# Placing score tiles by the matmuls of their own row half

## The chip, the cores and the metric

The kernel runs on one core of a Trainium2 chip. The metric is the device time of one execution in microseconds; the time before is the median of three runs.

## The reference

The input `x` has 2048 tokens of width 512. It is normalised per token (no scale, no shift), and two branches work on the result:

```python
xn = layernorm(x)
qkv = xn @ wqkv                        # 32 heads of width 16
s = softmax(q @ k.T / 4) @ v @ wo      # attention, then projection
g = silu(gelu(xn @ w1 + b1) @ w2 + b2) # 1376 hidden columns
out = x + s * g
```

All inputs are float32. The projections and both layers of the gated branch are made of three matmuls for each product: high times high, high times low, and low times high part of the operands.

## The kernel before, in words

The work runs in three parts, one after the other on TensorE.

The **first part** normalises `x`, transposes it, and makes some of the value and query/key tiles with 128-row matmuls.

The **middle part**, called the 64-row part here, makes the rest of the values, queries and keys and the whole gated branch. Its contractions are cut into halves of 64 rows: half 0 of the array (rows 0 to 63) and half 1 (rows 64 to 127) each take their own stream of matmuls, and both accumulate into the same PSUM tiles in turn. `run` issues these products in steps: in each step it raises `prog["n"]`, and for each half `a` it first calls `fill(a)` and then `mm(a, ...)`. There are 1488 steps, so each half gets 1488 product matmuls. A list `plan`, made ahead, orders the pieces: `quad` (values), `half` (first layer, queries and keys) and `down` (second layer).

`fill(a)` places the **score tiles**. Before the softmax can be taken, the row maxima of all scores are needed, and the kernel computes them in a pass of its own: `s_one(a)` takes the next tile for half `a`, `s_mm` makes 128 x 512 scores with one matmul of 48 rows in that half, and `s_max` reduces them on VectorE to two maxima per row. Such a tile takes one of two PSUM buffers (`ps_a`, `ps_b`) from the ring `s_ring`, in turn; a tile can be started when the reduction of the tile two before it has released the buffer. `4 * LEAD` = 576 score tiles are placed in the 64-row part, 288 on each half, half 0 and half 1 in turn (that is what `made[0] <= made[1]` decides). The remaining 1472 are made in the last part.

When 64 tiles of a unit (four heads, 512 queries) are done, `s_end0` reduces the maxima once more on VectorE, and some tiles later the place of one score tile is taken by `s_end1` and `s_end2`: a small transpose with all 128 rows in a buffer of the same ring (L252), a copy on ScalarE (L258), and a DMA on SP. This happens eight times in the 64-row part. `s_end0` also asks for the loads of queries two units ahead.

When a product accumulates into a PSUM tile that the other half wrote last, `mm` needs a proof that this write is over. `prog["seen"]` holds how far that is known: `taken()` raises it with each score tile (the third one back must be over), and where this is not enough, `mark()` puts a one-element instruction on ScalarE (L569) for which the matmul then waits. `SLOTS` = 1470 is the step at which the last score tile is to be placed, `FILL0` = 84 the step before which none is.

The **last part** runs the attention: transposed scores, exponentials on ScalarE, products with the values, the rest of the score tiles, and the output projection.

Of the kernel before, what the change touches and what calls it, by code (L numbers as in the profile page):

```python
# [32 lines left out]
LEAD = 144  # L33
# [3 lines left out]
FILL0 = 84  # L37
# [10 lines left out]
def fused(ctx: ExitStack, tc: tile.TileContext, x, wqk, wv, wo, w1, b1, w2, b2, out):  # L48
# [105 lines left out]
    made = [0, 0]  # L154
# [3 lines left out]
    def tick():  # L158
        for e in later:
            e[0] -= 1  # L160
# [31 lines left out]
    def s_whole(job, a):  # L192
        ps = s_tile()[0]
        s_mm(ps, job, a, 0, 0, CH)
        s_max(ps, job, a, slice(0, 2))

    def s_one(a):
        made[a] += 1
        s_whole(heads[made[a] - 1], a)
# [48 lines left out]
    prog = {}  # L248

    def s_end1(u):  # L250
        pm = s_tile()[0] if "seen" in prog else t_tile()
        nc.tensor.matmul(pm[:2 * GH * NCH, :P], NM.pop(u).rearrange("p i a -> p (i a)"), ident_r, start=True, stop=True)  # L252
        MH[u] = pm

    def s_end2(u):
        mh = qring.tile([2 * GH * NCH, P], F32, name="mh", bufs=1)
        if "seen" in prog:
            nc.scalar.activation(mh, MH.pop(u)[:2 * GH * NCH, :P], AF.Copy)  # L258
        else:
            nc.vector.tensor_copy(mh, MH.pop(u)[:2 * GH * NCH, :P])  # L260
        nc.sync.dma_start(mh_d[u].rearrange("i j (q s) -> (i j q) s", s=P), mh)
        sent.add(u)
# [33 lines left out]
    for j in range(len(pairs)):  # L296
        for h in range(2):
# [4 lines left out]
            due = next((i for i in range(j, len(pairs)) if is_m[i]), len(pairs))  # L302
# [4 lines left out]
            n = 2 if nd < len(parts) and parts[nd][2] and ready - nd > room else 1  # L307
            n = max(n, need - 2 * (left - 1))
# [215 lines left out]

    prog.update(n=0, pe=0, seen=0)
    writer = {}
    s_when = []
    ndown = sum(1 for e in plan if e[0] == "down")
    SLOTS = 12 * (4 * VQ + 2 * len(pairs)) + 6 * ndown - 18

    def fill(a):
        due = 4 * LEAD * (prog["n"] - FILL0) // (SLOTS - FILL0)
        if sum(made) < min(due, 4 * LEAD) and (made[0] <= made[1]) == (a == 0):
            taken()
            if later and later[0][0] <= 0:
                u = later.pop(0)[1]
                s_end1(u)
                s_end2(u)
                return
            s_one(a)  # L540
            tick()

    def taken():
        prog["pe"] += 1
        s_when.append(prog["pe"])
        if len(s_when) > 2:
            prog["seen"] = max(prog["seen"], s_when[-3])

    def mm(a, key, ps, lhs, rhs, first, last):
        r = slice(64 * a, 64 * a + 64)  # L550
        token = None
        if not first and writer[key][0] != a and writer[key][1] > prog["seen"]:
            if not tokens or tokens[-1][0] < writer[key][1]:
                mark()
            prog["seen"], token = next(x for x in tokens if x[0] >= writer[key][1])
        i = nc.tensor.matmul(ps, lhs[r], rhs[r], start=first, stop=last).ins  # L556
        if token is not None:
            tc.add_manual_dep(i, token, SYNC, reason="other row tile")
        prog["pe"] += 1
        latest[0] = (prog["pe"], i.name)  # L560
        writer[key] = (a, prog["pe"])

# [2 lines left out]
    def mark(dve=False):  # L565
        if dve:
            i = nc.vector.tensor_copy(junk[:, 1:], ident_r[:1, :1].bitcast(F32)).ins
        else:
            i = nc.scalar.activation(junk[:, :1], ident_r[:1, :1].bitcast(F32), AF.Copy).ins  # L569
        tc.add_manual_dep(i, latest[0][1], SYNC, reason="row tile done")  # L570
        tokens.append((latest[0][0], i.name))
# [7 lines left out]
    def run(ops, hooks={}):  # L579
        for n, two in enumerate(zip(*ops)):  # L580
            prog["n"] += 1
            for a in range(2):
                fill(a)
                mm(a, *two[a])
            for h in hooks.get(n, []):
                h()
# [321 lines left out]
    for t in range(NW):  # L908
        n = DONE + 2 * t
# [6 lines left out]
    for i, t in enumerate(late):  # L916
        n = L - 2 * len(late) - 1 + 2 * i
# [86 lines left out]
```

## Time and profile before

| | |
|---|---|
| median of 3 runs (lowest, highest) | 1636.11 us (1634.83, 1637.08) |
| the profiled execution: its time / its span | 1635.62 us / 1633.7 us |
| busy share of the span: TensorE, VectorE, ScalarE, GpSimd | 98%, 86%, 77%, 23% |
| granted TensorE clock | 0.998 |
| 64-row part: first and last product matmul | 52.9 us, 491.5 us |
| score tiles in it: number, first and last | 576, 72.7 us, 486.6 us |
| products of the 64-row part: mean record of a matmul | 0.39 us |

The record of a matmul lasts from its start to its modelled end; matmuls overlap, so the distance between starts, and not the record, tells the rate. L180 is the matmul of a score tile, L186 its reduction, L556 the products of the 64-row part, L252 the transpose of `s_end1`. PEld rows are weight loads; each matmul has its own.

### The profile page before, as it was taken

How to read it: one execution, taken by the hardware profiler on the slowest of the kernel's cores; microseconds unless marked ns; L12 is line 12 of the kernel's file. 1: busy time of each engine (PE TensorE's matmuls, PEld its weight loads, DVE VectorE, ACT ScalarE, POOL GpSimd, SP SyncE). 2: the span in 40 equal slices, each digit the busy share in tenths (PEclk: the TensorE clock that was granted, in tenths of full speed). 3: DMA queues.
4: the chain of work that ended last, by engine and by line, in shares of the span. 5: the costliest groups of instructions: out<-in, count | busy, mean ns of one | idle time of the engine just before them, and what ended most of it. 6: DMA issues, size and time to landing. Idle time of an engine off the chain costs nothing.

```text
span 1633.7 us, 32521 instructions
## 1 busy us (share of the span) xinstructions
PE 1605.2 (98%) x12146; PEld 928.8 (57%) x12146; DVE 1406.8 (86%) x2330; ACT 1255.7 (77%) x2522; POOL 371.8 (23%) x366
## 2 busy tenths in 40 slices
PE   9999999999999999999999999999999999999998
PEld 7899998999994444444444444444444444444445
DVE  7299999999988999999999999999999999999733
ACT  4333333434339999999999999999999999999884
POOL 4235565755640001001100200100010000000144
PEclk9999999999999999999999999999999999999999
DMA  6625333454322113111411411321131111110152
GB/s 200 148 65 156 103 127 97 146 143 123 110 82 72 41 28 70 29 35 40 78 32 26 67 41 28 59 39 29 34 69 27 28 29 41 29 32 18 57 191 94
DMA packets 76222, 116.93 MB, mean 72 GB/s; under 512 B 24964, under 2 KB 26244, under 8 KB 74696
## 3 DMA queue, kind: packets, MB, share of 16 engines
q1 hardware_dynamic: 72604, 102.42, 22.9%
q0 software_dynamic: 3264, 12.35, 3.9%
q8 instruction: 96, 1.57, 0.4%
q14 instruction: 62, 0.51, 0.1%
q10 hardware_dynamic: 196, 0.07, 0.0%
HBM read 84.35 MB, written 25.97 MB: 68 GB/s over the span
## 4 chain that ended last, share of the span: by engine, by line
PE 92%; ACT 4%; DVE 2%; issue 1%; DMA 0%; ACTq 0%; POOL 0%; SPq 0%; DVEq 0%; POOLq 0%
PE ps L773 21%; PE ps L180 14%; PE pst L704 14%; PE ps L556 12%; PE pv L773 8%; PE pst L556 7%; PE ps L704 5%; PE ps L79 3%; PE pv L180 3%; ACT slot L706 3%; PE pv L556 2%; PE pst L79 1%; DVE os L780 1%; ACT os L779 1%; DVE slot L74 0%
## 5 line engine op out<-in xcount | busy, mean ns | idle before, releaser
L186 DVE TENSOR_REDUCE mx<-ps 128x2 f32<-128x512 f32 x1685 | 1096.9, 685 | 121.7 <-PE ps L180 80.3
L706 ACT ACTIVATE slot<-pst 128x512 f32<-128x512 f32 x1533 | 833.7, 606 | 29.4 <-PE pst L704 18.2
L773 PE MATMUL ps<-slot,vsb 128*32 128x512 f32 x2944 | 392.1, 605 | 0.0
L704 PE MATMUL pst<-qt,kt 50*128 50x512 f32 x1149 | 378.2, 429 | 0.4 <-DVE gt L637 0.3
L180 PE MATMUL ps<-kt,slot 48*128 48x256 f32 (+1 forms) x1036 | 325.2, 374 | 8.2 <-DVE os L780 8.2
L706 ACT ACTIVATE slot<-ps 128x512 f32<-128x512 f32 x515 | 311.5, 606 | 21.0 <-PE pst L704 13.7
L704 PEld LDWEIGHTS pst<-qt,kt 50*128 50x128 f32 x1149 | 182.9, 184 | 243.2 <-ACT slot L706 239.1
L186 DVE TENSOR_REDUCE mx<-pv 128x2 f32<-128x512 f32 x363 | 248.1, 684 | 18.5 <-PE pv L180 14.0
L556 PE MATMUL ps<-slot,w1h 64*128 64x512 f32 x1088 | 234.2, 394 | 0.4 <-ACT junk L569 0.4
L180 PE MATMUL ps<-kt,qz 48*128 48x512 f32 x512 | 218.9, 429 | 0.3 <-ACT mh L258 0.3
L180 PEld LDWEIGHTS ps<-kt,slot 48*128 48x128 f32 x1036 | 170.3, 184 | 38.1 <-DVE os L780 15.2
L556 PEld LDWEIGHTS ps<-slot,w1h 64*128 64x128 f32 x1088 | 159.9, 185 | 9.1 <-ACT junk L569 1.9
L704 PE MATMUL ps<-qt,kt 50*128 50x512 f32 x387 | 162.7, 422 | 0.0
L556 PE MATMUL ps<-slot,w1l 64*128 64x512 f32 x544 | 159.7, 393 | 0.0
L773 PE MATMUL pv<-slot,vsb 128*32 128x512 f32 x1152 | 153.2, 604 | 0.8 <-DVE gx L866 0.8
L180 PE MATMUL ps<-slot,slot 48*128 48x256 f32 (+1 forms) x442 | 140.4, 375 | 3.7 <-DVE os L780 3.1
L360 POOL TENSOR_TENSOR hl<-hg,hh 128x512 fp32r<-128x512 f32 x76 | 96.8, 1295 | 135.7 <-ACT hh L359 79.9
L180 PE MATMUL pv<-kt,slot 48*128 48x512 f32 (+1 forms) x328 | 123.1, 375 | 3.1 <-DVE os L780 3.0
L569 ACT ACTIVATE junk<-ident_r 1x1 f32<-1x1 f32 x90 | 17.7, 196 | 134.1 <-PE pst L556 128.4
L704 PE MATMUL pst<-qt,slot 50*128 50x512 f32 x384 | 119.1, 423 | 0.0
L704 PEld LDWEIGHTS ps<-qt,kt 50*128 50x128 f32 x387 | 71.2, 184 | 67.5 <-ACT slot L706 52.8
L773 PEld LDWEIGHTS ps<-slot,vsb 128*32 128x32 f32 x2944 | 57.9, 108 | 84.0 <-issue 83.7
(165 smaller groups left out, 2085.5 us busy)
## 6 DMA issues: line engine op xcount, KB each, us to landing
raw<-in_w SPq DMA_DIRECT2D x88, 256.0 KB
qk_h<-hh SPq DMA_DIRECT2D x32, 256.0 KB
qk_l<-hl SPq DMA_DIRECT2D x32, 256.0 KB
qt<-qk_h SPq DMA_DIRECT2D x128, 64.0 KB
slot<-qk_h SPq DMA_DIRECT2D x92, 64.0 KB
xt<-in_x SPq DMA_DIRECT2D x16, 256.0 KB
g_d<-gt POOLq DMA_DIRECT2D x16, 256.0 KB, 3.7
qt<-qk_l SPq DMA_DIRECT2D x64, 64.0 KB
```

The costliest lines, as they stand in the source:

```text
L79: nc.tensor.matmul(ps, lhs[a], rhs[b], start=first and n == 0, stop=last and n == 2)
L180: return nc.tensor.matmul(ps[:, c0:c0 + w], QS[u][r, p, qi * P:(qi + 1) * P], kts[u // NCH % KB][p][r, k0:k0 + w], start=True, stop=True).ins
L186: nc.vector.tensor_reduce(MX[u][:, 2 * p:2 * p + 2, qi, ki][:, heads, parts], ps.rearrange("p (n c) -> p n c", c=HC), axis=AX.X, op=OP.max)
L360: nc.gpsimd.tensor_sub(hl, raw, hh.bitcast(F32))
L556: i = nc.tensor.matmul(ps, lhs[r], rhs[r], start=first, stop=last).ins
L569: i = nc.scalar.activation(junk[:, :1], ident_r[:1, :1].bitcast(F32), AF.Copy).ins
L704: nc.tensor.matmul(ps, kts[g % KB][p][r, k * P:(k + 1) * P], QT[u][r, p, :], start=True, stop=True)
L706: nc.scalar.activation(PT[u, k][:, 2 * p + a, :], ps, AF.Exp, scale=SCALE)
L773: nc.tensor.matmul(PV[u][32 * j:32 * j + 32, :], vsb[:, k, h:h + 32], PT[u, k][:, j, :], start=(k == 0), stop=(k == NT - 1))
L779: nc.scalar.activation(OS[u][:, :HC], pv[:, :HC], AF.Copy)
L780: nc.vector.tensor_copy(OS[u][:, HC:], pv[:, HC:])
```

## The change

`fill(a)` decides in a different unit when the next tile is due. Before, the number of tiles that should have been placed is worked out from the step: 576 spread evenly over the steps from 84 to 1470. After, `row[a]` counts every matmul given to half `a`, products and score tiles alike, and `put` counts the places taken (score tiles and the transposes of `s_end1`). A tile may be placed on half `a` when `row[a]` has reached a due count that starts at 84 and rises by (1470 + 288 - 84) / (576 + 9) = 2.86 with each place taken. The order of the halves, the number of tiles and their work stay as they are.

```diff
-    s_when = []
+    s_when, put, row = [], [0], [0, 0]
     ndown = sum(1 for e in plan if e[0] == "down")
     SLOTS = 12 * (4 * VQ + 2 * len(pairs)) + 6 * ndown - 18
 
     def fill(a):
-        due = 4 * LEAD * (prog["n"] - FILL0) // (SLOTS - FILL0)
-        if sum(made) < min(due, 4 * LEAD) and (made[0] <= made[1]) == (a == 0):
+        due = FILL0 + put[0] * (SLOTS + 2 * LEAD - FILL0) // (4 * LEAD + LEAD // 16)
+        if sum(made) < 4 * LEAD and row[a] >= due and (made[0] <= made[1]) == (a == 0):
             taken()
+            put[0] += 1
             if later and later[0][0] <= 0:
                 u = later.pop(0)[1]
                 s_end1(u)
                 s_end2(u)
                 return
             s_one(a)
+            row[a] += 1
             tick()
...
         prog["pe"] += 1
+        row[a] += 1
         latest[0] = (prog["pe"], i.name)
         writer[key] = (a, prog["pe"])
```

## The prediction

> **What bounds the kernel now.** I read the page first, for what is busy; then busy time by stretch and the chain, for the 64-row part; then the groups and waits of that part; then the timeline, one score tile at a time.
>
> ```profile
> PE 1605.2 (98%) x12146; PEld 928.8 (57%) x12146; DVE 1406.8 (86%) x2330; ACT 1255.7 (77%) x2522; POOL 371.8 (23%) x366
> ```
>
> ```profile
> 52.80:491.60 438.80, 438.17 (x3565) 397.19 (x3564) 383.34 (x597) 160.21 (x363) 237.55 (x203) 1.00 0.41 116
> ```
>
> ```profile
> 206.33 0.70 PE ps L556 x6
> ```
>
> TensorE never rests, and in the stretch of the 64-row part (second fence: PE, PEld, DVE, ACT, POOL) it is busy 438.17 of 438.80 us. That hides a loss. The two row halves run side by side: in the chain six products take 0.70 us, three for each half, so a matmul occupies its half for one slot of 0.233 us. Each half has 1488 products, 288 score tiles and 8 transposes of `s_end1`: 1784 slots, 416.3 us. The stretch is 438.8 us long. Each half loses 22.5 us in gaps that the other half covers, so no view of idle time shows them. The attention part follows in order on the same engine; a microsecond lost by both halves here moves the end by one.
>
> Where is it lost? The groups of the stretch in which score tiles are made, and the waits:
>
> ```profile
> L186 DVE TENSOR_REDUCE mx<-ps 128x2 f32<-128x512 f32 x576 | 378.9, 689 | 60.5 <-PE ps L180 35.8 <-PE ps L556 7.3 <-PE pst L556 4.9
> ...
> L180 PE MATMUL ps<-kt,qz 48*128 48x512 f32 x512 | 218.9, 429 | 0.3 <-ACT mh L258 0.3
> ```
>
> ```profile
> PEld ps L180 <- DVE mx L186: 4.2, 15, 0.3
> PEld ps L556 <- ACT junk L569: 1.9, 5, 0.8
> ```
>
> VectorE needs 378.9 us for its 576 reductions in 415 us: not the bound. But a score tile's record is 429 ns on average, where a product's is 390: some start before their weights are in. The timeline has the reason:
>
> ```profile
> 73.11 0.69 DVE L186 TENSOR_REDUCE mx<-ps 128x2 f32<-128x512 f32 x1 [28.61 <-PE ps L180]
> ...
> 75.92 1.43 DVE L186 TENSOR_REDUCE mx<-ps 128x2 f32<-128x512 f32 x2
> ...
> 200.23 1.29 DVE L186 TENSOR_REDUCE mx<-ps 128x2 f32<-128x512 f32 x2 [0.27 <-PE ps L556]
> ```
>
> ```profile
> 76.66 0.18 PEld L180 LDWEIGHTS ps<-kt,qz 48*128 48x128 f32 x1
> ```
>
> ```profile
> 72.69 0.39 PE L180 MATMUL ps<-kt,qz 48*128 48x512 f32 x1
> ...
> 73.15 0.39 PE L180 MATMUL ps<-kt,qz 48*128 48x512 f32 x1
> ...
> 74.09 0.39 PE L180 MATMUL ps<-kt,qz 48*128 48x512 f32 x1
> ...
> 74.60 0.50 PE L180 MATMUL ps<-kt,qz 48*128 48x512 f32 x1
> ...
> 75.49 0.39 PE L180 MATMUL ps<-kt,qz 48*128 48x512 f32 x1
> ...
> 76.11 0.39 PE L180 MATMUL ps<-kt,qz 48*128 48x512 f32 x1
> ...
> 76.66 0.50 PE L180 MATMUL ps<-kt,qz 48*128 48x512 f32 x1
> ...
> 77.50 0.40 PE L180 MATMUL ps<-kt,qz 48*128 48x512 f32 x1
> ...
> 79.64 0.49 PE L180 MATMUL ps<-kt,qz 48*128 48x512 f32 x1
> ...
> 80.94 0.49 PE L180 MATMUL ps<-kt,qz 48*128 48x512 f32 x1
> ```
>
> ```profile
> 480.23 0.41 PE L180 MATMUL ps<-slot,qz 48*128 48x512 f32 x1
> ...
> 481.06 0.39 PE L180 MATMUL ps<-slot,qz 48*128 48x512 f32 x1
> ...
> 481.66 0.41 PE L180 MATMUL ps<-slot,qz 48*128 48x512 f32 x1
> ...
> 482.47 0.39 PE L180 MATMUL ps<-slot,qz 48*128 48x512 f32 x1
> ...
> 482.98 0.49 PE L180 MATMUL ps<-slot,qz 48*128 48x512 f32 x1
> ...
> 484.48 0.40 PE L180 MATMUL ps<-slot,qz 48*128 48x512 f32 x1
> ...
> 485.27 0.44 PE L180 MATMUL ps<-slot,qz 48*128 48x512 f32 x1
> ...
> 485.88 0.43 PE L180 MATMUL ps<-slot,qz 48*128 48x512 f32 x1
> ...
> 486.62 0.49 PE L180 MATMUL ps<-slot,qz 48*128 48x512 f32 x1
> ```
>
> The tile at 75.49 is reduced from 75.92 for 0.69 us, to 76.61. The tile two later, at 76.66, takes the same buffer; its weight load starts at 76.66, 0.05 after the reduction, and the matmul with it. Its record is 0.50 instead of 0.39: the weights are 0.11 us late, and its half loses that. So a buffer is free 0.43 + 0.69 + 0.05 = 1.17 us after its tile's start at best, and the next user wants it 0.11 before its own slot, at 1.28. Two tiles that share a buffer sit on the same half. What matters is the number of own-half slots between them: 6 slots are 1.40 us, enough; 5 slots are 1.17 us, at least 0.11 short.
>
> **The change in counts.** Before, tiles are 1386/576 = 2.41 steps apart, so 2 or 3. In own-half slots that is 2 or 3 from a tile of half 0 to one of half 1, and one more (3 or 4) on the way back, because the tile of half 0 counts itself. After, each place is 2.86 slots after the last one, both ways: mostly 3, sometimes 2, never 4. Stepping both rules through the plan gives, for each tile, the last two distances:
>
> - 3 and 3: 216 before, 397 after
> - 2 then 4, 4 then 2: 117 and 117 before, none after
> - 2 then 3: 54 before, 81 after; 3 then 2: 54 before, 80 after
> - at a transpose of `s_end1`: 24 before (distances 3, 4, 0, 3) and 24 after (3, 5, 2, 3)
>
> The old rule looks rougher, but a 2 is mostly followed by a 4: again 6 slots, the half's reuse distance is kept. Only 108 tiles have 5. The new rule is more even, yet 161 tiles have 5. The reason is in the mean: 2.86 against 2.91, since the transposes now get full distances of their own and the tiles between them move together.
>
> **The prices.** For every score tile of the trace I take the time from the matmul before it on its half to the one after it, less two slots. The quoted rows are the first and the last of each group (two before, one after: 72.69 to 74.09, 480.23 to 481.66 for 2 then 4; 73.15 to 74.60, 481.06 to 482.47 for 4 then 2; 75.49 to 76.66, 481.66 to 482.98 for 2 then 3; 76.11 to 77.50, 484.48 to 485.88 for 3 and 3; 79.64 to 80.94, 485.27 to 486.62 for 3 then 2). The means: 3 and 3, 0.035 us (216 tiles); 2 then 4, 0.020 (101) and 4 then 2, 0.007 (101); 2 then 3, 0.205 (54); 3 then 2, 0.202 (54). Apart stand the 32 tiles just behind a unit's end, 4.4 us in all:
>
> ```profile
> 118.83 0.29 DVE L238 TENSOR_REDUCE nmh<-mx 128x16 fp32r<-128x128 f32 x1
> 119.03 0.28 DVE L238 TENSOR_REDUCE nm<-mx 128x16 f32<-128x128 f32 x1
> ```
>
> These two reductions push back the ones behind them, eight times, under either rule: 4.4 us stay. The 24 places around the transposes cost 2.1 us:
>
> ```profile
> 126.58 0.25 PE L252 MATMUL ps<-ident_r,nmh 128*32 128x128 f32 x1
> ```
>
> ```profile
> 126.87 0.27 ACT L258 ACTIVATE mh<-ps 32x128 f32<-32x128 f32 x1 [1.52 <-PE ps L252]
> ```
>
> The transpose's buffer is free 0.56 us after its start (127.14). Before, the next user comes 3 slots (0.70) later, after it 5 slots (1.17); the other two reuse distances become 8 and 7. So these 2.1 us go, if ScalarE answers as here; if not, up to 2.1 come back.
>
> Before, both halves together: 216 x 0.035 + 101 x 0.020 + 101 x 0.007 + 54 x 0.205 + 54 x 0.202 + 4.4 + 2.1 = 38.6 us, of the 45 lost. After: 365 x 0.035 (32 of the 397 stand for the tiles behind unit ends) + 81 x 0.205 + 80 x 0.202 + 4.4 = 49.8 us.
>
> Waits for the other half's writes rise from 12 to 15 (ScalarE marks from 90 to 93, hidden: ScalarE is busy 160 of 439 us). By the waits view four of them took 1.9 - 0.8 = 1.1 us, 0.28 each; three more cost 0 to 0.8 us, I take 0.4. `s_end1` and `s_end2` come five steps earlier, with their DMA and the query loads that `s_end0` asks for on SP, which are used two units (about 308 steps) later: nothing. The first tile comes two steps earlier, 0.47 us at most if its operands have just landed; the last four earlier, and nobody waits for its buffer before step 1482: nothing. The clock stays at 1.00.
>
> Sum: 49.8 + 0.4 - 38.6 = 11.6 us over both halves, and as neither half can run away from the other, 5.8 us for each. The profiled execution took 1635.6 us (span 1633.7), so 1641.4 by its own time; the median of the runs shown is 1636.1, 0.5 higher: **1641.9 us**.
>
> Bounds: a tile with 5 slots costs at least 0.11 (worked out above) and at most about 0.25 (79.64 to 80.94 is 1.30, 0.14 past 5 slots, and 0.11 for the weights); one with 6 slots costs between 0 and, in the mean, 0.035.
>
> **Rivals.** *Even arrivals are what VectorE needs (faster).* Reductions of 0.64 us each (two in 1.29) fit into even distances of 0.70, the queue on VectorE is gone, every release comes at 1.17: 5 slots cost 0.11, 6 nothing. Then 161 x 0.11 + 4.4 = 22.1 against 38.6, 8.2 us less for each half: 1627.9. It decides if releases come by 1.17. Against it: 3 and 3 occurs 216 times now, and costs 0.035 there.
>
> *Runs of threes become cheap (no difference).* A 2 now makes both halves late in turn, and the threes behind it start with slack, like the 2 and 4 pairs now (mean 0.0135). Then 365 x 0.0135 + 32.8 + 4.4 + 0.4 = 42.5, 2.0 us per half: 1638.1.
>
> *Place in the stream decides (slower yet).* If the halves did not run ahead of each other, a tile of half 1 would start a slot later than counted: real distances of 4 and 2, or 2 then 1 for the 36 tiles of half 0 that come 2 after one of half 1. Those 36 reductions would wait 0.64 - 0.23 = 0.41 us, so the release comes at 1.58 and the next user is 0.18 + 0.11 late instead of 0.035: 36 x 0.255 = 9.2; some 215 others wait 0.17 and cost 0.05: 3.2. That is 6.2 more per half: 1648.1. Against it: between the tiles at 72.69 and 73.15 (half 0 and half 1) stand three products of half 0 in program order, so strict order would put them three slots (0.70) apart; they are two apart (0.46). The Trainium skill ("TensorE: Matmul & The Clock Gate", section "The mechanism") holds that matmuls start in strict program order, whatever their row group; by that rule this rival would be the forecast, and these two rows speak against it.
>
> **How the numbers follow.** The forecast has 0.60, the faster rival 0.10, the cheap threes 0.22, the stream order 0.08. A measurement of this kernel can tell about 0.2% (3.3 us) from no change: 1632.8 to 1639.4. Faster is the first rival: 0.10. Same is the cheap threes and a tenth of the forecast: 0.28. Slower: 0.62. The range leaves out the faster rival and part of the last one, and takes in the bounds of the two main prices: 1635 to 1648.
>
> **What would show it.** In the changed profile: the stretch to the last L556 row ends some 6 us later than 491.5, and the attention part is as long as before; score tiles in runs of about 0.70 with a pair of late ones (record 0.50) every seven; the mean record of L180 rises above 429; behind the L252 rows no late tiles. The forecast is wrong if the mean record of L180 falls, if the threes stay at records of 0.39, or if the change of time lies outside the 64-row part.

## The result and the profile after

| | before | after |
|---|---|---|
| median of 4 runs each (lowest, highest) | 1636.23 us (1634.83, 1637.08) | 1646.88 us (1644.90, 1647.15) |
| the profiled execution: its time / its span | 1635.62 / 1633.7 us | 1647.15 / 1645.2 us |
| first and last product of the 64-row part | 52.89, 491.55 us | 53.37, 502.87 us |
| from the last product's start to the end | 1142.2 us | 1142.3 us |

The changed kernel is slower: ratio 1.0063, 95% interval 1.0046 to 1.0081, 10.65 us by the medians. In the code after, products are L558, the marks L572; L180 (score tile), L186 (reduction), L238 (unit end) and L252 (transpose) keep their numbers.

The page's first part, then busy time by stretch for the 64-row part (PE, PEld, DVE, ACT, POOL; granted clock, DMA):

```profile
PE 1612.6 (98%) x12146; PEld 920.2 (56%) x12146; DVE 1398.9 (85%) x2330; ACT 1256.5 (76%) x2525; POOL 372.2 (23%) x366
```

```profile
53.30:502.90 449.60, 445.91 (x3565) 389.80 (x3564) 375.80 (x597) 160.67 (x366) 237.63 (x203) 1.00 0.40 113
```

TensorE is idle for 3.7 us of the stretch (0.6 before) and the clock is 1.00, but the stretch is 449.6 us long where it was 438.8, with the same number of matmuls. So most of the loss is again in gaps of one half that the other half covers. The whole difference lies here, but for the products starting 0.48 us later; the attention part is as long as before. Counted much as in the prediction (each half's time from the start of its first product to that of its last, less 1783 distances of 0.233 us), a half lost 23.1 us before and loses 34.0 now.

The groups of that stretch:

```profile
L186 DVE TENSOR_REDUCE mx<-ps 128x2 f32<-128x512 f32 x576 | 371.5, 687 | 78.0 <-PE ps L180 42.2 <-PE ps L558 15.2 <-PE pst L558 4.7
...
L180 PE MATMUL ps<-kt,qz 48*128 48x512 f32 x512 | 222.4, 438 | 2.9 <-DVE mx L186 2.2 <-DMA qz<-qk_h 0.7
```

The mean record of a score tile is 438 ns (before 429), as the forecast wanted. The row above it holds something that the prediction did not read, although it stood in its own quotation: idle time of the reductions is ended by products (`ps L558` and `pst L558`; L556 in the kernel before), whose results they don't read. It was 7.3 + 4.9 us before and is 15.2 + 4.7 now. That row turned out to be the key.

### The profile page after: what moved, and what is told of

It reads as the page before. It is cut to its first block, busy times and chain, and to the rows that moved or that the text cites. A ratio compares the mean times of both kernels' runs of the same rounds, so it can differ in the third digit from the quotient of the medians.

```text
span 1645.2 us, 32526 instructions
## 1 busy us (share of the span) xinstructions
PE 1612.6 (98%) x12146; PEld 920.2 (56%) x12146; DVE 1398.9 (85%) x2330; ACT 1256.5 (76%) x2525; POOL 372.2 (23%) x366
## 4 chain that ended last, share of the span: by engine, by line
PE 91%; ACT 4%; DVE 3%; issue 1%; DMA 0%; ACTq 0%; POOL 0%; SPq 0%; DVEq 0%; POOLq 0%
PE ps L776 21%; PE ps L180 14%; PE pst L707 14%; PE ps L558 12%; PE pv L776 8%; PE pst L558 7%; PE ps L707 5%; PE pv L180 3%; ACT slot L709 3%; PE ps L79 3%; PE pv L558 2%; PE pst L79 1%; DVE os L783 1%; DVE mx L186 1%; ACT os L782 1%
## 5 line engine op out<-in xcount | busy, mean ns | idle before, releaser
L186 DVE TENSOR_REDUCE mx<-ps 128x2 f32<-128x512 f32 x1685 | 1090.0, 685 | 138.9 <-PE ps L180 85.5
L180 PE MATMUL ps<-kt,slot 48*128 48x256 f32 (+1 forms) x1036 | 325.4, 375 | 8.2 <-DVE os L783 8.2
L186 DVE TENSOR_REDUCE mx<-pv 128x2 f32<-128x512 f32 x363 | 248.4, 684 | 18.4 <-PE pv L180 13.9
L558 PE MATMUL ps<-slot,w1h 64*128 64x512 f32 x1088 | 230.0, 395 | 0.4 <-ACT junk L572 0.4
L180 PE MATMUL ps<-kt,qz 48*128 48x512 f32 x512 | 222.4, 438 | 2.9 <-DVE mx L186 2.2
L180 PEld LDWEIGHTS ps<-kt,slot 48*128 48x128 f32 x1036 | 170.2, 184 | 38.2 <-DVE mx L186 15.2
L558 PEld LDWEIGHTS ps<-slot,w1h 64*128 64x128 f32 x1088 | 155.6, 185 | 10.2 <-ACT junk L572 3.1
L558 PE MATMUL ps<-slot,w1l 64*128 64x512 f32 x544 | 149.5, 393 | 0.0
L180 PE MATMUL ps<-slot,slot 48*128 48x256 f32 (+1 forms) x442 | 140.5, 375 | 3.7 <-DVE os L783 3.1
L572 ACT ACTIVATE junk<-ident_r 1x1 f32<-1x1 f32 x93 | 18.2, 196 | 147.7 <-PE pst L558 139.4
L180 PE MATMUL pv<-kt,slot 48*128 48x512 f32 (+1 forms) x328 | 123.1, 375 | 3.2 <-DVE os L783 3.1
L180 PEld LDWEIGHTS ps<-kt,qz 48*128 48x128 f32 x512 | 93.6, 183 | 28.7 <-DVE mx L186 13.2
```

What stands on the lines that cost most here:

```text
L180: return nc.tensor.matmul(ps[:, c0:c0 + w], QS[u][r, p, qi * P:(qi + 1) * P], kts[u // NCH % KB][p][r, k0:k0 + w], start=True, stop=True).ins
L186: nc.vector.tensor_reduce(MX[u][:, 2 * p:2 * p + 2, qi, ki][:, heads, parts], ps.rearrange("p (n c) -> p n c", c=HC), axis=AX.X, op=OP.max)
```

## The experiments

Two theories stood at the start. **A**, the prediction's: what costs is a buffer used again after too few own-half slots (5), dearest behind a unit's end, where two more reductions stand in VectorE's row. **B**: the place in program order decides (a tile and the next of its buffer stand 8, 4 or 2 matmuls apart in the stream).

### Where the short distances fall

The first kernel shifts the phase of the due count, so that behind every unit's end stand two distances of 3:

```diff
-        due = FILL0 + put[0] * (SLOTS + 2 * LEAD - FILL0) // (4 * LEAD + LEAD // 16)
+        due = FILL0 + (put[0] * (SLOTS + 2 * LEAD - FILL0) + 284) // (4 * LEAD + LEAD // 16)
```

> Same rule, same spacing, only the rounding of the due count is shifted (+284 of 585), so that the 16 tiles two and three behind a unit's end all come 3 own-half slots apart; there are as many short distances elsewhere (73 against 72 pairs of 3-2 and 2-3). Theory A (short reuse distances, dearest where they meet the two extra reductions of a unit's end): the 8 tiles that are 0.72 us late in the changed kernel and the products of half 1 held behind them cost 14.3 us over both halves there and about 6 here: 4 us less per half than the changed kernel, about 1643. Theory B (what counts is the place in the program's order, distances of 8 and 4 matmuls): the order is the same, 1646.9.

Measured: 1644.66 us, ratio 1.0050 (1.0036 to 1.0063), between the two theories, and 2.2 us below the changed kernel by the medians; the intervals of the two ratios overlap. The next two carry the same number of short distances, all ahead of half 1 or all ahead of half 0:

```diff
+    gap, due = [-360], [FILL0]
+    def next_due():
+        places = 4 * LEAD + LEAD // 16
+        gap[0] += SLOTS + 2 * LEAD - FILL0 - 3 * places
+        two = gap[0] <= -places and (made[0] <= made[1]) == (1 == 0)   # (0 == 0) in the other
+        gap[0] += places * two
+        due[0] += 3 - two
...
-        if sum(made) < 4 * LEAD and row[a] >= due and (made[0] <= made[1]) == (a == 0):
+        if sum(made) < 4 * LEAD and row[a] >= due[0] and (made[0] <= made[1]) == (a == 0):
```

> As the phase-shifted kernel, but a distance of 2 slots is only ever given ahead of a tile of half 1 (73 of them). Theory A: no product of the other half is held behind a late tile (loss of half 1's products about 1 to 2 us instead of 10), but the following tile of half 0 then pays its full price (0.24 instead of 0.15): about 1643, within 1.5 us of the phase-shifted kernel. Theory B: no tile follows two matmuls behind another, distances 8, 6 and 4: 4 to 5 us less than the phase-shifted kernel.

> The counterpart: a distance of 2 slots only ahead of a tile of half 0 (73 of 3-2, 81 of 2-3), which is then two matmuls behind its predecessor in the program. Theory A: half 1's products lose 7 us more behind late tiles, the tiles of half 1 pay less (0.15): about 1644, within 1.5 us of the kernel with the short distances on half 1. Theory B: 73 tiles at 0.255 us more, about 9 us slower than that kernel.

Measured: 1643.87 us, ratio 1.0043 (1.0030 to 1.0055), and 1648.41 us, ratio 1.0073 (1.0060 to 1.0086). The two should have agreed by A and differ by 9 us by B; they differ by 4.5, and neither theory holds as it stood. The distances are the same, so it matters ahead of which half they stand. In the traces half 1's products lose some 5 to 6 us in the first and 13 to 14 in the second, there more than half of it beside score tiles of half 0 that wait for their buffer.

Then the same short distances ahead of half 1 with the transposes not counted as places, which leaves 116 reuses of 5 slots (the changed kernel has 161):

```diff
-        places = 4 * LEAD + LEAD // 16
+        places = 4 * LEAD     # and no next_due() where a transpose takes the place
```

> The changed rule with the transposes not counted as places, as before the change: the tile behind a transpose comes at once, the others 2.906 own-half slots apart; short distances only ahead of half 1, none at a unit's end. 5-slot reuses: 116 (before 108, changed kernel 161), everything else even. Theory A: 442 x 0.031 + 54 x 0.22 + 62 x 0.23 + about 7 for unit ends and transposes = 47 us against 38.6 before: 1639 to 1640. Theory B: the program's order is still 8 and 4 nearly everywhere: 1644 or more.

Measured: 1642.42 us, ratio 1.0041 (1.0029 to 1.0054), between what A and B wanted. With nearly as few 5-slot reuses as the kernel before (108), it is still 5.5 us slower than that. A alone doesn't explain that.

### Shorter reductions

Here both kernels have reductions in the 64-row part that read half of each tile's columns (the other half is left out of those maxima, and the exponentials of nine units are scaled):

```diff
+        src = ps.rearrange("p (n c) -> p n c", c=HC)
+        if "seen" in prog:
+            src = src[:, :, :HC // 2]
```

> The changed kernel, but in the 64-row part each reduction reads only half of the columns of its score tile (half of the maxima are left out; the exponentials of these nine units are scaled down so that they stay finite, which moves no time). A buffer is then free about 0.43 + 0.37 + 0.05 = 0.85 us after its tile's start, before the 1.06 at which a tile 5 slots later wants it. Theory A (short reuse distances cost because the buffer is not free): all of these prices vanish, some 29 us less: about 1617 to 1619, equal to the kernel of before with the same edit within 1.5 us. Theory B (the place in the program's order costs in itself): the order is unchanged, a difference of 5 us or more to the kernel of before with the same edit stays.

> The kernel before with the same edit (half of the maxima of the 64-row part left out). Theory A: about 18 us less, 1617 to 1619, the same as the changed kernel with this edit. Theory B: faster than that by 5 us or more.

Measured: the changed kernel with this edit 1620.76 us, ratio to the kernel before 0.9913 (0.9900 to 0.9927); the kernel before with it 1617.74, ratio 0.9891 (0.9877 to 0.9904). The group of the changed kernel in the 64-row part, where the reduction has become L189:

```profile
L189 DVE TENSOR_REDUCE mx<-ps 128x2 f32<-128x256 f32 x576 | 241.5, 424 | 182.9 <-PE ps L180 133.7 <-PE ps L561 20.0 <-PE pst L561 8.7
L180 PE MATMUL ps<-kt,qz 48*128 48x512 f32 x512 | 191.4, 399 | 1.5 <-DMA qz<-qk_h 1.0 <-ACT mh L261 0.5
```

The reduction takes 424 ns where it took 687, the tile's record falls to 399, and the difference of the two rules from 10.7 to 3.0 us. A 5-slot reuse now costs about 0.02 us and no longer 0.21, though its distance is the same 1.17 us. So the loss does pass through the release of the buffer. B, which wanted 5 us or more, falls. A, which wanted the two within 1.5 us of each other, misses too: in these traces the 32 tiles behind unit ends still cost 5.9 us over both halves under the new rule, and 0.8 under the old one.

### One reduction less at a unit's end

In both kernels the second of the two L238 reductions becomes a copy on ScalarE:

```diff
-        for dst in (NM[u][:, 0], nm):
-            nc.vector.tensor_reduce(dst, mx, axis=AX.X, op=OP.max, negate=True)
+        nc.vector.tensor_reduce(nm, mx, axis=AX.X, op=OP.max, negate=True)
+        nc.scalar.activation(NM[u][:, 0], nm, AF.Copy)   # in the 64-row part
```

> The kernel before; at a unit's end in the 64-row part the second of the two extra reductions on VectorE is replaced by a copy on ScalarE. Theory A: the 32 tiles behind unit ends and the products held behind them cost 5.4 us over both halves now, about 1.5 then: 2 us less, about 1634.5. If unit ends were not a place where time is lost: no change.

> The changed kernel with that same replacement. Theory A: the late tile behind each unit's end (0.72 us on half 0, with half 1 held behind it) is 0.28 earlier on both halves: 14.3 us become about 7, 3.5 us less for each half: about 1643.5. If the unit ends have no part in what the change cost beyond the forecast: 1646.9.

Both missed: 1635.73 us, ratio 1.0002 (0.9993 to 1.0011), and 1647.42 us, ratio 1.0073 (1.0060 to 1.0085). Starts of these small reductions lie 0.20 us apart (119.45, 119.65, 119.85 below), so the copy saves 0.20 us and not 0.28, and the price of the late tile falls only from 0.83 to 0.60 us. By the traces the 64-row part is shorter by 0.35 us in the kernel before and by 0.5 in the changed one, and the time outside the span has grown by 0.4 us in both (2.4 where it was 2.0). So unit ends do cost time, but taking off part of that cost gave much less than the price of the late tile alone would; why is not shown.

### The same count, another pattern

Here the due count still runs in own-half matmuls, but rises by 2 ahead of half 1 and by 4 (116 times 3) ahead of half 0. A second kernel also puts the last tile five steps later:

```diff
+    def next_due():
+        places = 4 * LEAD
+        if made[0] > made[1]:
+            due[0] += 2
+            return
+        gap[0] += 2 * (SLOTS + 2 * LEAD - FILL0) - 6 * places
+        three = gap[0] <= -places
+        gap[0] += places * three
+        due[0] += 4 - three
...
-    SLOTS = 12 * (4 * VQ + 2 * len(pairs)) + 6 * ndown - 18
+    SLOTS = 12 * (4 * VQ + 2 * len(pairs)) + 6 * ndown - 13   # the second kernel only
```

> The count by own-half matmuls stays, but the due count rises by 2 ahead of half 1 and by 4 ahead of half 0 (116 times by 3), and the transposes take no distance of their own. That gives 442 tiles with distances 2 and 4 in turn, 116 tiles with 5 slots to the tile two before, and only 2-4 pairs behind a unit's end. Theory A (only the slots between two users of one buffer count): 442 x 0.0135 + 54 x 0.23 + 62 x 0.20 = 30.8, unit ends 4.4 to 5.5, transposes and the tiles behind them 2 to 4: 37 to 40 us over both halves against 38.6 to 40 before, so -1.5 to +1 us for each: 1634.5 to 1637.5 us. If counting by own halves in itself cost something (the tile lands at another place in the step than before, or queries and marks fall elsewhere), the time stays above 1641, like the other versions with this count.

> As the other kernel of this call, with the place of the last tile five steps later (SLOTS 1475), so 101 tiles with 5 slots and not 116. Theory A: 15 x 0.2 = 3 us less over both halves, 1.5 us for each, against the other kernel: 1633 to 1636 us, if nothing in the attention part waits for the last tile; if something there does, up to 5 x 0.233 = 1.2 us come back.

Measured: 1631.08 us, ratio 0.9971 (0.9959 to 0.9983), and 1630.67 us, ratio 0.9969 (0.9958 to 0.9981). Both beat the kernel before, which A did not foresee; that the second gains over the first can't be told. The count by own halves is thus no loss in itself; the pattern of twos and fours is better than the even threes by 11.3 us (against 1642.42 with as many, 116, short reuses). The groups of the first:

```profile
L186 DVE TENSOR_REDUCE mx<-ps 128x2 f32<-128x512 f32 x576 | 388.4, 690 | 45.8 <-PE ps L180 35.6 <-PE ps L569 1.4
L180 PE MATMUL ps<-kt,qz 48*128 48x512 f32 x512 | 213.6, 419 | 1.4 <-ACT mh L258 0.9 <-DMA qz<-qk_h 0.4
```

Here products (L569 in this code) end only 1.4 us of the reductions' idle time. The 5-slot reuses cost 0.153 us each where they cost 0.21, and reductions end on average 1.20 us after their tile's start, where the threes of the changed kernel have 1.29. Why should they be earlier?

### A tile's end is reported in program order

The timeline of the changed kernel, two tiles and what stands between (start, duration):

```profile
85.37 0.40 PE L180 MATMUL ps<-kt,qz 48*128 48x512 f32 x1
85.49 0.39 PE L558 MATMUL pst<-kt,slot 64*128 64x512 f32 x1
...
85.96 0.39 PE L180 MATMUL ps<-kt,qz 48*128 48x512 f32 x1
```

```profile
85.95 2.67 DVE L186 TENSOR_REDUCE mx<-ps 128x2 f32<-128x512 f32 x4 [0.27 <-PE pst L558]
```

The tile at 85.37 belongs to half 1. The product at 85.49 belongs to half 0 and was issued just ahead of it; the tile overtook it by 0.12 us. VectorE is idle, but the reduction starts at 85.95: 0.58 after its tile, 0.46 after the product, which the trace names as what released it. Over all tiles of this kernel whose reduction found VectorE idle: where all earlier-issued matmuls had started 0.2 us ahead of the tile or more, the reduction starts 0.43 us after it (17 tiles, 0.425 to 0.435). Where one started about 0.10 later, it starts after 0.58 (42 tiles); about 0.15 later, after 0.60 (127 tiles); about 0.20 later, after 0.66 (30 tiles). Matmuls of two halves may start out of program order, but their ends are reported in it.

It could be that the reduction only waits for a count of finished matmuls that takes in the product as well, and that the tile's own end is reported in time. The trace also holds the times at which TensorE raises that count. It is raised at 85.895, 0.40 us after the product's start, and at 85.929, 0.56 after the tile's; at 85.37 + 0.40 there is nothing. A tile that overtakes nothing raises it 0.40 us after its start (the one at 85.96 does so at 86.36). In this kernel 122 tiles overtake by more than 0.02 us with their weights in time: for each the count goes up 0.40 us after the start of the overtaken matmul, and once more 0.034 us later; at 0.385 to 0.425 us after the tile's own start it goes up in only 2 of the 122. So it is the tile's own report that comes late.

In the changed kernel 216 of the 288 tiles of half 1 overtake a product of half 0, because `run` issues the step's product of half 0 ahead of the tile of half 1. Reductions end at 1.29 on average and not at 1.12 (0.43 and 0.69), and 0.05 more until the next weight load makes 1.34: past the 1.28 that a 6-slot reuse leaves. In the kernel before, 128 tiles of half 1 and 104 of half 0 overtake; in the two-and-four kernel 134 and 83, on half 1 by less than half as much (mean over its tiles 0.041 us against 0.106). Over the tiles of both halves together the kernel before overtakes about as far as the changed one (mean 0.055 and 0.058 us). So late reports should cost the kernel before, too, and not only explain what the change added.

The test moves the tile ahead of that product and leaves the distances between tiles as they are:

```diff
             for a in range(2):
                 fill(a)
+            for a in range(2):
                 mm(a, *two[a])
```

> The changed kernel, but each step places score tiles for both halves first and issues its two products behind them; the own-half distances of all tiles stay exactly the same (397 with 3 and 3, 161 with 5 slots). Theory P (a score tile's end is reported in program order): in the changed kernel 216 of 288 tiles of half 1 start ahead of the product of half 0 issued before them, and their reductions start 0.60 us after the tile and not 0.43; issued ahead of that product, they needn't wait for it. Releases come at about 1.19 and not 1.29, prices fall to those of the two-and-four kernel (0.0065 and 0.153): 381 x 0.0065 + 145 x 0.153 + 8 at unit ends, and half the held products: some 42 us over both halves where it was 68, so 1634 us, between 1631 and 1639. Theory D (the own-half distances alone decide): the prices stay, 1646 us, less up to 1 us for eight fewer waits for the other half.

> The kernel before with the same edit; its distances stay too (216 with 3 and 3, 234 with 2 and 4, 108 with 5 slots). In it 128 tiles of half 1 and 104 of half 0 start ahead of a product issued before them. Theory P: those of half 1 no longer wait, those of half 0 may; prices fall towards 0.0065 and 0.153, 434 x 0.0065 + 108 x 0.153 + 6 = 25 us where it was 38.6, so some 5 to 7 us less: 1629 to 1632; the two rules then differ by 3 to 6 us and no longer by 10.7. Theory D: 1636, and the difference stays at 10.

Measured: the changed kernel 1631.84 us, ratio to before 0.9974 (0.9964 to 0.9984); the kernel before 1624.80 us, ratio 0.9932 (0.9918 to 0.9945). The two edited lines take 15 us from the one and 11 from the other, for the first within what was expected (1631 to 1639), for the second more, and the old rule with this order is the fastest of the kernels with full reductions. The groups of the 64-row part, of the changed kernel with the edit, then of the kernel before with it:

```profile
L186 DVE TENSOR_REDUCE mx<-ps 128x2 f32<-128x512 f32 x576 | 376.0, 689 | 57.4 <-PE ps L180 40.6
L180 PE MATMUL ps<-kt,qz 48*128 48x512 f32 x512 | 214.5, 419 | 3.1 <-DVE mx L186 2.0 <-DMA qz<-qk_h 1.1
```

```profile
L186 DVE TENSOR_REDUCE mx<-ps 128x2 f32<-128x512 f32 x576 | 379.7, 690 | 49.7 <-PE ps L180 34.9 <-PE pst L556 0.7
L180 PE MATMUL ps<-kt,qz 48*128 48x512 f32 x512 | 212.1, 414 | 0.4 <-ACT mh L258 0.4
```

The products are gone from the reductions' idle time (0 and 0.7 us). No tile of half 1 overtakes by more than 0.02 us any more, and the reductions of idle VectorE start 0.43 to 0.46 us after their tiles. The timeline shows the difference at a glance; the changed kernel, and the same with the edit:

```profile
88.81 2.66 DVE L186 TENSOR_REDUCE mx<-ps 128x2 f32<-128x512 f32 x4 [0.18 <-PE pst L558]
91.65 3.98 DVE L186 TENSOR_REDUCE mx<-ps 128x2 f32<-128x512 f32 x6 [0.19 <-PE pst L558]
95.91 2.68 DVE L186 TENSOR_REDUCE mx<-ps 128x2 f32<-128x512 f32 x4 [0.28 <-PE pst L558]
```

```profile
87.78 24.65 DVE L186 TENSOR_REDUCE mx<-ps 128x2 f32<-128x512 f32 x36
```

In this window (88 to 112 us) thirty-six reductions follow each other without a hole, one every 0.685 us. The prices fall to 0.001 us for 3 and 3 (from 0.031) and 0.11 for a 5-slot reuse (from 0.21), which is the bound that the prediction had worked out, the late weights alone.

Between the two rules 7.0 us are left by the medians (5.1 by the profiled executions, 1631.57 and 1626.48). So a third of the difference (over half of it by the profiled executions: 5.1 of 11.5 are left) hangs on the order of issue, and the rest stays with the rule. Theory D, the distances alone, falls. That A explains all the rest is not shown: up to 1.1 us of it is TensorE's wait for a load of queries (`DMA qz<-qk_h` in the rows of the changed kernel, missing from those of the other), and reuses of 5 slots away from unit ends, tiles behind unit ends and products held by the other half are each dearer under the new rule in these two traces, with no run that takes them apart.

## Why the prediction was right, and where it was short

Direction and place came as forecast: the 64-row part is longer, everything else as before, the reason is the buffer of a score tile, and the counts were exact. The forecast said 5.8 us for each half, the measurement 10.65. That 1646.88 us still lies in the stated range is luck in part: with all 161 reuses of 5 slots at their upper bound of 0.25 us the prediction's sum gives some 3.7 us more, 1645.6, and what went beyond the forecast came from other terms. The sums over both halves from the trace after stand below, against the prediction's terms (with its prices as printed these add up to 38.8 and 49.9 and not 38.6 and 49.8; the difference between the rules is the same):

| term | before | forecast after | trace after |
|---|---|---|---|
| 6-slot reuses away from unit ends | 10.1 | 12.8 | 11.7 (381 x 0.031) |
| 5-slot reuses | 22.0 | 32.6 | 30.9 (73 x 0.205 + 72 x 0.221) |
| 32 tiles behind unit ends | 4.4 | 4.4 | 9.2 |
| 24 places at transposes | 2.1 | 0 | 0.3 |
| all other losses, held products among them | 7.5 | 7.9 | 15.9 |
| sum | 46.1 | 57.7 | 68.0 |

**The prices held** away from unit ends: a reuse of 5 slots cost 0.213 us where 0.203 was forecast, on the 145 of the 161 that this row holds. The other sixteen stood behind unit ends, and there the first step failed.

**"4.4 us stay."** They became 9.2. The tile with a 5-slot reuse sits right behind the unit's end in the new pattern, eight times out of eight, where the old one had a 2 then 4. VectorE, then TensorE (PEld: its weight load):

```profile
119.45 0.29 DVE L238 TENSOR_REDUCE nmh<-mx 128x16 fp32r<-128x128 f32 x1
119.65 0.28 DVE L238 TENSOR_REDUCE nm<-mx 128x16 f32<-128x128 f32 x1
119.85 1.96 DVE L186 TENSOR_REDUCE mx<-ps 128x2 f32<-128x512 f32 x3
```

```profile
118.73 0.43 PE L180 MATMUL ps<-kt,qz 48*128 48x512 f32 x1
...
120.58 0.18 PEld L180 LDWEIGHTS ps<-kt,qz 48*128 48x128 f32 x1 [0.81 <-DVE mx L186]
120.58 0.49 PE L180 MATMUL ps<-kt,qz 48*128 48x512 f32 x1 [0.38 <-DVE mx L186]
```

The buffer of the tile at 118.73 is wanted 5 slots later, at 119.90, and used at 120.58. Such a tile costs 0.83 us, eight times 6.6 us, where the prediction's upper bound for a reuse of 5 slots was 0.25. (One of the eight, at 167.96, also waited for a load; see below.) The prediction had taken all 32 tiles behind unit ends for threes; sixteen of them have 5 slots. The shifted kernel, with 3 and 3 there, is 7.7 us above the kernel before and not 10.65, though the intervals of the two ratios overlap.

**A term that was missing: products held by the other half.** At 120.59 a product of half 1 starts too, held as long as the tile of half 0:

```profile
120.59 0.72 PE L558 MATMUL ps<-slot,w1l 64*128 64x512 f32 x2
```

Half 1's products lost about 1.5 us before and lose about 10 now, some 8 of it beside late tiles of half 0, some 5 of that at the eight unit ends. The prediction let the two halves wait apart from each other. Short distances ahead of half 1 alone (1643.87 us) against half 0 alone (1648.41) agree with this; in their traces the score tiles cost about the same (50.8 and 49.3 us over both halves), so the difference lies between products. Those kernels also differ in how far half 1 overtakes (mean 0.079 and 0.132 us), so the 4.5 us between them aren't shown to come from the distances alone.

**"These 2.1 us go."** They did at the transposes (0.3). Small beside the rest.

**Waits for writes, and a load that was put at nothing.** The forecast took 0.4 us for three more waits for the other half's writes; the weight loads' part in the waits view is 3.1 us (nine) where it was 1.9 (five), 1.2 more:

```profile
PEld ps L558 <- ACT junk L572: 3.1, 9, 0.8
...
PE ps L180 <- DMA qz<-qk_h: 0.7, 1, 0.7
```

The last of these lines is a term that the prediction put at nothing: the query loads that `s_end0` asks for. It took them to be used two units (about 308 steps) later, but the loads asked for at the end of the first unit are needed 64 tiles later, when the third unit starts. The tile at 167.96 is one of its first:

```profile
167.96 0.51 PE L180 MATMUL ps<-kt,qz 48*128 48x512 f32 x2 [0.69 <-DMA qz<-qk_h]
```

All of TensorE stands for 0.69 us until its queries have landed, and the two tiles there cost 1.29 and 0.96 us in the row of the 32 tiles. The kernel before has no such wait. The very first tile (72.71) waited for nothing.

**The rivals.** Even arrivals brought VectorE nothing: the threes' reductions ended at 1.29 and not at 1.12. Threes did not become cheap either (0.031). The stream order was the rival nearest to the time, 1648.1, but in its own form, strict order of the starts, it is refuted: at 85.37 and 85.49 two matmuls start against program order. That its time came nearer than the forecast's says nothing for its mechanism. The Trainium skill ("TensorE: Matmul & The Clock Gate", section "The mechanism") holds that they start in strict order; the trace disagrees by these rows. What keeps the order is the report of the end. With the tile issued ahead of the product, the first rival's prices (0.11 for 5 slots, next to nothing for 6) are what the runs show.

**Left open.** Why even threes drive half 1 ahead of half 0, and twos and fours do not: in steps where both halves have had equally many tiles, half 1's product starts 0.31 us after that of half 0 in the kernel before, 0.145 in the changed one, 0.24 in the two-and-four kernel (medians). Late tiles shift this, and it decides how far tiles overtake, but no run set it by itself. Nor was the reorder tried with the two-and-four pattern.

## What to carry to other kernels

When a consumer starts late, look at what the trace names as its releaser: if it is a matmul whose result it doesn't read, the cause may be the order of issue. Moving the needed matmul ahead cost two lines here and no extra work. An even spacing is no aim by itself; count the distance between two users of one buffer, and see what happens where the shortest distance meets the consumer's own interruptions. Where two streams share a queue, one stream's wait has a price in the other that an account by stream leaves out.

## What the runs showed of the hardware

Two matmuls on different row halves start out of program order, but the end of one is reported only when the earlier-issued one is over too: a consumer starts 0.43 us after the start of a matmul that overtook nothing, and 0.60 after that of one that overtook by 0.15. The late report follows that of the overtaken matmul by 0.034 us (all 122 cases looked at in the changed kernel's trace). A score tile that waits for its buffer holds products of the other half that come behind it (120.58 and 120.59). Back-to-back reductions of 0.69 us start 0.61 to 0.68 us apart, the 0.28 us ones 0.20, so here the duration of a record overstates how long the next instruction has to wait behind it.
